# A chunked RWKV-5 mixer with a normalised MLP: r loaded four tokens a partition and turned for four batches at once, k turned alone by DMA, loads issued from two queues

## The chip, the cores and the metric

The kernel runs on one core of a Trainium2 chip. That core has a matrix engine (TensorE, PE in the profile; PEld is its loading of weights), three engines for elementwise work (VectorE or DVE, ScalarE or ACT, GpSimd or POOL), a queue engine (SyncE, SP) and 16 DMA engines. The metric is the device time of one launch in microseconds (us), the median of several runs.

## What is computed

Inputs are r, k and v of shape (4 batches, 8 heads, 768 tokens, 48), a decay w and a bonus u per head and dimension, and two matrices of an MLP that widens 384 to 1536 and back. The reference, cut to what matters:

```python
for t in range(S):
    cur = einsum('bhd,bhe->bhde', u * k[t], v[t])
    y[t] = einsum('bhd,bhde->bhe', r[t], state + cur)
    state = w * state + einsum('bhd,bhe->bhde', k[t], v[t])
...
mu, var = mean(x), mean((x - mu)**2)          # x is y with the heads side by side
xn = (x - mu) / sqrt(var + 1e-6) * g_ln
out = x + maximum(xn @ w_ch1, 0) @ w_ch2
```

The output is (4, 768, 384) in float32.

## The kernel before

The 768 tokens are cut into six chunk rows of 128. A tile is one chunk of one batch, 128 tokens by 8 heads by 48; there are 24, and tile i is chunk row i // 4 of batch i % 4. Inside a chunk the recurrence becomes matrix products: with r of token t scaled by w^t and k by w^-(t+1), the product of the scaled k and r, masked to earlier tokens, weighs v; the state Z at the start of the chunk is multiplied by the scaled r; and the token's own term comes from u.

The steps of a tile, by the names in the code:

- LR, LK, LV load r, k, v of a tile (L326, L323, L329), tokens on the partitions. One piece of memory is the 48 numbers of one head of one token, 192 bytes.
- SR and SK scale r and k by the tables Fr and Fk (tile `sc` in the profile); CV casts v to bf16 (`vv`).
- The scaled r and k must be turned, so that the dimension lies on the partitions (`trs`). Tiles 0 to 7 do it on PE: TR (L345) makes eight 128x128 transposes, four of r and four of k, into PSUM (`tr`), and TCr and TCk, or TC for both, copy them out. Tiles 8 to 23 do it by one DMA transpose of r and k together, TKR (L490).
- Q multiplies the turned r and k (`q`). AT (L364) forms the products (`at`), AM masks them (`A`). S computes the token's own weights (L395), for tiles 4 to 7 adds the old state by an identity matmul (L402), and makes the state product (L408); ZU and ZD make the next state Z. CC copies the own weights (`cc`), VB multiplies v by them (`Vb`). Y sums the state's part (L437) and the masked part (L445); X adds Vb (`x`) and gives the row sum.
- SQ and RS make the norm's factor, XN the centred rows (`xn`). They are turned for the MLP (`xT`): tiles 0 to 5 by LT on PE (L505) and a copy XT, tiles 6 to 19 two at a time by a DMA transpose LT2 (L484), the last four by LTD (L480).
- UP (L520) is a quarter or half of a widening product into one of two PSUM buffers (`hp`), RL (L536 on ACT, L538 on DVE) the relu out of it (`hT`). MLP groups have one or two tiles; a UP of one tile has 12 matmuls of 128 columns, of two tiles 6 to a matmul group of 256 columns. DN (L548) is a third of the narrowing product, four matmuls of 384 columns (`o`). OT adds x, STO stores. The last tile's narrowing is made in halves (DA, DB, L563).
- LW1, LW2 load the two weight matrices in thirds (`w_f`, L298 and L315; LW2 n into the buffer of LW1 n), SW scales and casts the first, CW casts the second.

At the start WF loads w to all partitions, LN takes its logarithm, FR and FK make the tables by exponentials, and WL makes the decay of a whole chunk, again by a logarithm and an exponential. TL (L229) loads in advance an activation table set named for both functions. DU and WU are matmuls on zeros that keep PE busy (L261, L265); a DU of n lasts as long as n matmuls of 128 columns.

The order is one written list, PLAN: each entry is a step, its number, and its engine (v DVE, s ACT, g POOL; for a DMA s means issued by ACT and - by SP). Every engine runs its entries in that order, and each waits only for its data and for its buffers. Tiles of one name form a ring (SLOTS: `kf`, `rf` and `vf` have eleven buffers each). In the list before, SP issues 123 DMAs, all loads among them; ACT issues 11.

Of the kernel before, what the change touches and what calls it, by code (L numbers as in the profile page):

```python
# [7 lines left out]
FP32 = mybir.dt.float32  # L8
BF16 = mybir.dt.bfloat16
ALU = mybir.AluOpType  # L10
# [5 lines left out]
K_BY_DMA = [8, 9, 10, 11, 12, 13, 14, 15, 16, 17, 18, 19, 20, 21, 22, 23]  # L16
SLOTS = {'kf': 11, 'rf': 11, 'vf': 11, 'sc': 3, 'vv': 4, 'trs': 3, 'q': 2, 'A': 2, 'cc': 4, 'Z': 6, 'ZS': 2, 'Vb': 3, 'x': 13, 'xn': 4, 'xT': 4, 'hT': 4, 'ot': 4}
PLAN = """
MP,0,v LR,1,- WF,0,s MW,0,v MI,0,g LR,0,- MM,0,g TL,0,s LC,1,- LK,0,- LV,0,- LN,0,s FR,0,s LC,0,s LR,2,- LK,1,- LC,2,s
SR,0,v FK,0,s SK,0,v LK,3,- DU,40,- CT,0,- TR,0,- CV,0,v LK,2,- SR,1,v TCr,0,s CP,0,v TCk,0,v UW,0,g LV,1,- UGC,0,s WL,0,s  # L20
DU,6,- AT,0,- Q,0,v SK,1,v S,0,- LW1,0,- SR,2,v TR,1,- LV,2,- CC,0,s SK,3,g AMb,0,v LR,3,- TCr,1,s AMa,0,v ZU,0,v VB,0,g
TCk,1,v DU,4,- Y,0,- SK,2,g CV,1,s DU,3,- AT,1,- X,0,v LW1,1,- Q,1,g AMb,1,v TR,2,- LW1,2,- AMa,1,v TCk,2,s LV,3,- DU,10,-
S,1,- TCr,2,s XN,0,v SW,2,v SW,0,s DU,5,- AT,2,- LR,4,- CC,1,v Q,2,v Y,1,- AMb,2,v LT,0,- CV,2,s VB,1,g SQ,0,s XT,0,v
SW,1,g X,1,v ZU,1,v SR,3,g XN,1,s DU,26,- UP,0,- AMa,2,v LT,1,- S,2,- RL,0,s SW,5,g XT,1,v ZU,2,v SW,3,s DU,5,- TR,3,-
Y,2,- LK,4,- RS,0,g CC,2,v SW,4,v TCr,3,s VB,2,v DU,4,- UP,1,- X,2,v SW,7,s LW2,0,- SW,6,g UP,17,- TCk,3,v LV,4,- RL,1,s
XN,2,v AT,3,- SW,8,s Q,3,v LW2,1,- UP,16,- CV,3,v RL,17,s LW2,2,- S,3,- SR,4,g RL,16,v DU,2,- UP,2,- LK,5,- AM,3,v CC,3,s
SQ,1,s SK,4,g LT,2,- UP,18,- XT,2,s RL,2,s ZU,3,v RS,1,g TR,4,- LR,5,- RL,18,s VB,3,v UP,34,- CW,1,s TC,4,v CW,0,g Y,3,-
UP,32,- X,3,v CV,4,s AT,4,- Q,4,v RL,32,s DN,4,- AM,4,v XN,3,g RL,34,s S,4,- LR,6,- SQ,2,s LT,3,- UP,33,- CC,4,v XT,3,v
CW,3,s VB,4,v Y,4,- RL,33,v UP,49,- CW,2,s X,4,v UP,50,- CW,4,s LK,6,- XN,4,v DN,5,- CW,5,v RL,49,s LR,7,- LT,4,- SK,5,v
RL,50,s DN,6,- XT,4,v SR,5,v UP,48,- LV,5,- OT,1,v TR,5,- SK,6,v ZU,4,v LK,7,- SR,6,g DN,0,- TC,5,s DN,1,- LV,6,- AT,5,-  # L30
Q,5,g TR,6,- LV,7,- AM,5,v UP,64,- DN,2,- TC,6,s LR,8,- CV,5,g SR,7,v RL,48,s AT,6,- S,5,- LR,9,- OT,0,v SQ,4,s SK,7,g
Y,5,- CC,5,s RL,64,s DN,8,- LK,8,- AM,6,v VB,5,g TR,7,- RS,2,g LK,9,- UP,65,- UP,66,- Q,6,v TC,7,s X,5,v ZU,5,v DN,9,-
CV,7,g LV,8,- RL,66,s CV,6,g AT,7,- SQ,3,s RS,4,g XN,5,v LV,9,- Q,7,v S,6,- SR,8,v LT,5,- LR,10,- DN,10,- ZU,6,v SK,8,g
CC,6,s SQ,5,s RL,65,s XT,5,v Y,6,- STO,0,s AM,7,v S,7,- UP,81,- VB,6,g TKR,8,- LK,10,- SK,9,g OT,2,v UP,80,- CC,7,v X,6,v
SR,9,g DN,16,- RL,80,v XN,6,s Y,7,- CV,8,s RS,5,g DN,17,- VB,7,v TKR,9,- RL,81,s STO,1,- X,7,v CV,9,g DN,18,- ZU,7,v SQ,7,s
XN,7,g UP,82,- OT,4,v Q,8,g LT2,6,- AT,8,- RL,82,s DN,20,- LK,11,- AM,8,v LR,11,- SK,10,g S,8,- DN,21,- CC,8,s RS,3,g Y,8,-
SR,10,v AT,9,- LV,10,- TKR,10,- DN,22,- VB,8,g UP,97,- OT,5,v Q,9,g LR,12,- UP,100,- ZU,8,v RL,97,s X,8,v DN,12,- SK,11,g SQ,6,s
AM,9,v LK,12,- S,9,- RL,100,s SR,11,g XN,8,s UP,99,- DN,13,- STO,2,- CC,9,s RL,99,s RS,6,g VB,9,v TKR,11,- Y,9,- ZD,8,v LV,11,-
AT,10,- UP,96,- ZU,9,v Q,10,g X,9,v DN,14,- RL,96,v UP,98,- XN,9,g OT,3,v CV,10,s LT2,8,- UP,101,- RL,98,s AM,10,v SK,12,g STO,3,-
DN,28,- LR,13,- S,10,- Q,11,v DN,29,- RL,101,v CC,10,s VB,10,g CV,11,s AT,11,- ZU,10,v LK,13,- LV,12,- Y,10,- SR,12,g AM,11,v DN,30,-  # L40
UP,115,- TKR,12,- X,10,v S,11,- LR,15,- RL,115,s UP,116,- CC,11,v OT,7,v XN,10,s VB,11,g LK,14,- Y,11,- RL,116,v DN,24,- SR,13,g X,11,v
CV,12,s SQ,8,s UP,112,- UP,117,- SQ,9,s XN,11,g RL,117,v ZD,9,g LT2,10,- DN,25,- RL,112,v LR,14,- AT,12,- SK,13,g LV,13,- DN,26,- UP,113,-
Q,12,v TKR,13,- ZU,11,v SK,14,g UP,114,- RL,113,s LK,15,- STO,4,- OT,6,v S,12,- RL,114,s UP,132,- CC,12,v SQ,11,s VB,12,g DN,32,- LV,14,-
RL,132,s RS,7,g SR,14,v UP,128,- UP,133,- SQ,10,s AM,12,v LV,15,- ZD,11,g DN,33,- RL,128,s LK,16,- Q,13,v AT,13,- STO,5,s ZD,10,v DN,34,-
RL,133,s SK,15,g ZU,12,v Y,12,- CV,13,s TKR,14,- UP,129,- OT,8,v SR,15,g X,12,v S,13,- LR,16,- DN,36,- CC,13,v CV,14,s AM,13,v ZU,13,v
UP,131,- TKR,15,- XN,12,s RL,131,s RL,129,s SQ,12,s DN,37,- STO,6,- VB,13,g ZD,12,g Y,13,- RS,8,g DN,38,- CV,15,v X,13,v UP,130,- OT,9,v
XN,13,s AT,14,- Q,14,v RL,130,s DN,40,- LT2,12,- AM,14,v SQ,13,s SR,16,g LV,16,- S,14,- DN,41,- LK,17,- CC,14,s STO,7,s ZU,14,v RS,9,g
Y,14,- SK,16,v AT,15,- Q,15,v DN,42,- TKR,16,- AM,15,v ZD,14,g VB,14,g S,15,- LR,17,- UP,149,- CC,15,s ZD,13,g OT,10,v UP,145,- RL,149,s
LR,18,- X,14,v VB,15,g DN,44,- RL,145,v XN,14,s UP,148,- ZU,15,v CV,16,s LV,17,- Y,15,- SQ,14,s DN,45,- SK,17,v RL,148,s LK,18,- X,15,v
AT,16,- ZD,15,g DN,46,- SQ,15,s UP,144,- Q,16,v XN,15,s OT,11,v SR,17,g UP,147,- RL,144,s LT2,14,- AM,16,v S,16,- UP,146,- TKR,17,- CV,17,g  # L50
STO,9,- RL,147,v DN,52,- RL,146,s LK,19,- SK,18,v Y,16,- CC,16,s LR,19,- ZU,16,v DN,53,- SR,18,v UP,161,- ZD,16,v DN,54,- VB,16,v RL,161,s
# [600 lines left out]
```

## Time and profile before

| | before |
|---|---|
| median of 3 runs | 154.89 us (153.79 to 155.48) |
| profiled execution: span from first to last instruction | 156.2 us |
| busy PE, DVE, POOL, ACT | 139.4, 112.9, 87.9, 75.1 us |
| DMA packets | 104465, of which 99579 under 512 bytes |
| first UP | 20.46 us |
| granted clock of PE | 1.00 throughout |

The span is that of one profiled execution; the runs are timed without a profile, and no other time is given for the profiled one. A group of the profile names line, engine, operation and tiles, then the count, the busy time, the mean in ns, and the idle time before it with what ended it. The chain of waits follows the last instruction back to what released it; SPq and ACTq stand for time in which a queue was issuing. A matmul's busy time overlaps that of its neighbours, so the distance from one start to the next is what a step costs when PE streams.

### The profile page before, as it was taken

How to read it: one execution, taken by the hardware profiler on the slowest of the kernel's cores; microseconds unless marked ns; L12 is line 12 of the kernel's file. 1: busy time of each engine (PE TensorE's matmuls, PEld its weight loads, DVE VectorE, ACT ScalarE, POOL GpSimd, SP SyncE). 2: the span in 40 equal slices, each digit the busy share in tenths (PEclk: the TensorE clock that was granted, in tenths of full speed). 3: DMA queues.
4: the chain of work that ended last, by engine and by line, in shares of the span. 5: the costliest groups of instructions: out<-in, count | busy, mean ns of one | idle time of the engine just before them, and what ended most of it. 6: DMA issues, size and time to landing. Idle time of an engine off the chain costs nothing.

```text
span 156.2 us, 4227 instructions
## 1 busy us (share of the span) xinstructions
PE 139.4 (89%) x1676; PEld 106.5 (68%) x1676; DVE 112.9 (72%) x224; ACT 75.1 (48%) x167; POOL 87.9 (56%) x127
## 2 busy tenths in 40 slices
PE   5659998999999869969969989998997999979991
PEld 1146687886778558757947767786775777758881
DVE  2149899996989856957659998899786767644421
ACT  3424666993766317135736547344253446615130
POOL 3016596503889979639739885134929885651000
PEclk9999999999999999999999999999999999999999
DMA  4999999988999979989989999999999898831221
GB/s 86 201 211 274 265 310 254 408 171 164 203 191 189 235 142 241 162 186 234 176 196 228 225 175 203 176 215 175 213 217 183 200 221 181 186 110 54 76 84 67
DMA packets 104465, 30.03 MB, mean 192 GB/s; under 512 B 99579, under 2 KB 102910, under 8 KB 104446
## 3 DMA queue, kind: packets, MB, share of 16 engines
q1 hardware_dynamic: 103132, 28.09, 89.4%
q10 hardware_dynamic: 1314, 1.67, 3.4%
q8 instruction: 13, 0.21, 0.6%
q14 instruction: 6, 0.05, 0.1%
HBM read 19.08 MB, written 4.72 MB: 152 GB/s over the span
## 4 chain that ended last, share of the span: by engine, by line
PE 29%; DMA 26%; SPq 21%; DVE 9%; POOL 5%; issue 4%; ACT 4%; ACTq 1%; DVEq 0%; POOLq 0%
PE hp L520 10%; PE o L548 9%; DMA xT<-xn 8%; DMA rf<-in_r_dram 8%; SPq L326 7%; SPq L329 5%; SPq L323 4%; DMA out_dram<-ot 3%; DMA w_all<-in_w_dram 2%; DMA kf<-in_k_dram 2%; DVE A L374 2%; POOL sc L194 2%; PE at L364 2%; PE o L261 2%; PE y L445 1%
## 5 line engine op out<-in xcount | busy, mean ns | idle before, releaser
L520 PE MATMUL hp<-xT,w_sb 128*128 128x128 bf16 (+1 forms) x612 | 57.1, 241 | 3.5 <-DMA xT<-xn 3.4
L548 PE MATMUL o<-w_sb,hT 128*128 128x384 bf16 x276 | 55.4, 326 | 0.6 <-DVE ot L604 0.4
L520 PEld LDWEIGHTS <-w_sb 128*128 128x128 bf16 x612 | 48.7, 114 | 8.4 <-DMA xT<-xn 3.2
L536 ACT ACTIVATE hT<-hp 128x512 bf16<-128x512 f32 x54 | 31.6, 595 | 34.4 <-PE hp L520 34.2
L548 PEld LDWEIGHTS <-hT 128*128 128x128 bf16 x276 | 24.2, 97 | 12.0 <-issue 0.8
L374 DVE TENSOR_TENSOR A<-at,mask 128x1024 bf16<-128x1024 f32 (+1 forms) x27 | 29.5, 1099 | 2.4 <-PE at L364 2.3
L194 POOL TENSOR_TENSOR sc<-kf,Fk 128x384 bf16<-128x384 f32 x15 | 15.4, 1026 | 14.9 <-DMA kf<-in_k_dram 9.0
L194 POOL TENSOR_TENSOR sc<-rf,Fr 128x384 bf16<-128x384 f32 x15 | 15.5, 1035 | 12.2 <-DMA rf<-in_r_dram 12.2
L604 DVE SCALAR_TENSOR_TENSOR ot<-o,rs,x 128x384 f32<-128x384 f32 x23 | 14.1, 614 | 8.7 <-PE o L548 4.3
L452 DVE SCALAR_TENSOR_TENSOR x<-y,Vb 128x384 f32<-128x384 f32 x24 | 13.2, 551 | 4.2 <-PE y L445 2.8
L427 POOL TENSOR_TENSOR Vb<-vf,cc 128x384 f32<-128x384 f32 x15 | 12.8, 850 | 6.0 <-DVE cc L191 4.3
L459 ACT ACTIVATE sqj<-x,sm 128x384 bf16<-128x384 f32 x24 | 14.7, 613 | 1.9 <-DVE x L452 1.8
L538 DVE TENSOR_SCALAR hT<-hp 128x512 bf16<-128x512 f32 x18 | 12.3, 686 | 3.1 <-PE hp L520 2.8
L364 PE MATMUL at<-trs 48*128 48x128 bf16 x192 | 10.0, 226 | 3.0 <-DMA trs<-sc 2.5
L476 POOL TENSOR_TENSOR rs<-rs,expo 128x1 f32<-128x1 f32 (+1 forms) x17 | 11.0, 649 | 1.4
L364 PEld LDWEIGHTS <-trs 48*128 48x128 bf16 x192 | 5.6, 97 | 8.6 <-DMA trs<-sc 3.9
L261 PE MATMUL o<-warm 128*128 128x512 bf16 x23 | 9.4, 533 | 2.0 <-DVE warm L226 2.0
L189 ACT CAST vv<-vf 128x384 bf16<-128x384 f32 x13 | 6.6, 509 | 9.2 <-DMA vf<-in_v_dram 7.8
L194 DVE TENSOR_TENSOR q<-trs 128x512 bf16<-128x512 bf16 x16 | 8.9, 555 | 2.6 <-DMA trs<-sc 2.5
L189 ACT COPY trs<-tr 128x512 bf16<-128x512 bf16 (+1 forms) x8 | 5.9, 747 | 9.3 <-PE tr L345 7.6
L194 POOL TENSOR_TENSOR q<-trs 128x512 bf16<-128x512 bf16 x8 | 9.6, 1196 | 0.9 <-PE hp L520 0.8
L445 PE MATMUL y<-vv,A 128*128 128x48 bf16 x192 | 8.8, 185 | 0.6 <-ACT vv L189 0.4
(76 smaller groups left out, 168.2 us busy)
## 6 DMA issues: line engine op xcount, KB each, us to landing
rf<-in_r_dram SPq DMA_DIRECT2D x24, 192.0 KB, 3.6
kf<-in_k_dram SPq DMA_DIRECT2D x24, 192.0 KB, 4.0
vf<-in_v_dram SPq DMA_DIRECT2D x24, 192.0 KB, 4.3
w_f<-in_moe_w_ch_dram SPq DMA_DIRECT2D x6, 768.0 KB, 6.1
out_dram<-ot SPq DMA_DIRECT2D x16, 192.0 KB, 3.6
out_dram<-ot ACTq DMA_DIRECT2D x7, 192.0 KB, 3.6
trs<-sc SPq DMA_TRANSPOSE x16, 3.5
w_all<-in_w_dram ACTq DMA_DIRECT2D x1, 192.0 KB, 3.8
```

Source lines behind the costliest of these rows:

```text
L189: nc.scalar.copy(out=out, in_=in_)
L194: engines[e].tensor_tensor(out=out, in0=in0, in1=in1, op=ALU.mult)
L261: nc.tensor.matmul(out=warm_ps[0][:], lhsT=warm[:], rhs=warm[:].unsqueeze(1).to_broadcast([P, 4, P]), start=True, stop=True)
L364: nc.tensor.matmul(out=t[:, par, q, :], lhsT=trs(i)[p0 : p0 + D, 1, q, :], rhs=trs(i)[p0 : p0 + D, 0, q, :], start=True, stop=True,)
L374: nc.vector.tensor_tensor(out=AA(i)[:, a:b].rearrange("p e q t -> p (e q) t"), in0=psum["at", i][:, a:b].rearrange("p e q t -> p (e q) t") ...
L427: engines[e].tensor_tensor(out=Vb(i)[:].rearrange("p (h d) -> p h d", h=H), in0=vf(i)[:], in1=cc(i)[:].unsqueeze(2).to_broadcast([P, H, D] ...
L452: nc.vector.scalar_tensor_tensor(out=xx(i)[:], in0=psum["y", i][:, :C], scalar=1.0, in1=Vb(i)[:], op0=ALU.mult, op1=ALU.add, accum_out=sm[ ...
L459: nc.scalar.activation(out=sqj[:], in_=xx(i)[:], func=ACT.Square, bias=sm[i][:], scale=-float(C), accum_out=sq[g][:, j : j + 1])
L520: nc.tensor.matmul(out=t[:, a * gw : (a + 1) * gw].rearrange("p (j t) -> p j t", j=size), lhsT=w1_sb[n][kc][:, fb::FB], rhs=xT(g)[:, :size ...
L536: nc.scalar.activation(out=o, in_=s, func=ACT.Relu)
L548: nc.tensor.matmul(out=psum["o", i][:, :C], lhsT=hT(g)[:, fk, j * P : (j + 1) * P], rhs=w2_sb[d][:, a, :], start=(fk == 0), stop=(fk == FK ...
L604: nc.vector.scalar_tensor_tensor(out=ot(i), in0=psum["o", i][:, :C], scalar=rs[g][:, j : j + 1], in1=xx(i)[:], op0=ALU.mult, op1=ALU.add,)
```

## The change

For chunk rows 1 to 5 (R_PACKED), r of the four batches of a row goes into one tile `rp`. LRP loads one batch into every fourth partition, four successive tokens of a head as one piece of 768 bytes. Four SRP scale it, two heads at a time over all four batches, by a new table Fr4, which FR4 makes in four exponentials out of `pow4`, the token numbers that MP4 computes on POOL in four small operations. Two TRP of eight transposes turn a whole row of r: the identity is read with a step of four, so that the batches come out apart; two TCP copy the result out of PSUM and put the tokens in order, into `rT`. k is scaled by SK as before and turned alone: on PE by TK (four transposes) for tiles 4 to 7, by TKD, one DMA transpose a tile, for tiles 8 to 23. Q, AT and Y read r from `rT` and k from `trk`. Row 0 keeps LR, SR and TR.

Loads may now be issued by ACT. The parts of a narrowing product may come in any order. The rings change: `kf` and `vf` 10, `rf` 4, `rp` 1, `rps` 1, `rT` 2, turned k 6, scaled k 6. The whole PLAN is new; its list gives SP 65 DMAs and ACT 69 (19 LK, 16 LV, 10 LRP, 3 LR, 3 LW1, 2 LW2, 13 STO and three more). The table load TL stands at the end of the list instead of near its start. On DVE, ACT and POOL some steps change places as well.

```diff
-K_BY_DMA = [8, 9, 10, 11, 12, 13, 14, 15, 16, 17, 18, 19, 20, 21, 22, 23]
+R_PACKED = [1, 2, 3, 4, 5]
...
+MI,0,g MP4,0,g MM,0,g WF,0,s MW,0,v LK,0,s LR,0,s LK,1,s DU,40,- LC,2,- MP,0,v DU,4,- DU,2,- LC,0,- LR,1,s LN,0,s FR,0,s FK,0,s SR,0,v SK,0,v LR,2,-
+LC,1,- LK,2,s LV,1,s TR,0,- CT,0,- FR4,0,s DU,6,- CP,0,s TCk,0,v SK,1,g LR,3,s TCr,0,v DU,5,- DU,3,- SR,1,v Q,0,v UW,0,g SR,2,g LV,0,- AT,0,- WL,0,s
+CV,0,s AMb,0,v AMa,0,v TR,1,- TCk,1,v S,0,- SK,2,v LRP,6,- LK,4,s TCr,1,s Q,1,v LW1,1,s AT,1,- TR,2,- Y,0,- FR4,1,s CC,0,s FR4,2,s LK,3,- CV,1,g
+ZU,0,v AMb,1,v VB,0,g FR4,3,s S,1,- TCk,2,v SR,3,g SK,3,g AMa,1,v TCr,2,s LV,2,- X,0,v ZU,1,v CC,1,s LRP,5,- AT,2,- Y,1,- VB,1,g TR,3,- LW1,0,s
...
+DA,2,- STO,22,- OA,23,v SA,23,s TL,0,s
...
+    def rTq(i, q):
+        return rT(i // B)[:, q, i % B, :] if i // B in R_PACKED else trr(i)[:, q, :]
...
+    def FR4(j, e):
+        nc.scalar.activation(out=Fr4[:, :, j, :], in_=ln_all[:], func=ACT.Exp, scale=pow4[:, j : j + 1])
...
     def LK(i, e):
-        nc.sync.dma_start(out=kf(i)[:], in_=chunk_src(k, i))
+        issuer(e).dma_start(out=kf(i)[:], in_=chunk_src(k, i))
...
+    def LRP(i, e):
+        c, b = divmod(i, B)
+        issuer(e).dma_start(
+            out=rp(c)[:].rearrange("(p b) h x -> b p h x", b=B)[b],
+            in_=r[b, :, c * L : (c + 1) * L, :].rearrange("h (p j) d -> p h (j d)", j=PK),
+        )
+
+    def SRP(i, e):
+        c, q = divmod(i, HP)
+        times(
+            e,
+            rps(c)[:, q].rearrange("p j (e x) -> p e j x", e=2)[:, :, :, :D],
+            rp(c)[:, 2 * q : 2 * q + 2].rearrange("p e (j d) -> p e j d", j=PK),
+            Fr4[:, 2 * q : 2 * q + 2],
+        )
+
+    def TRP(i, e):
+        c, h = divmod(i, 2)
+        t = psum["trp", i] = ps.tile([P, HP // 2, PK, P], BF16, name="tr")
+        for a in range(HP // 2):
+            for j in range(PK):
+                nc.tensor.transpose(
+                    out=t[:, a, j, :], in_=rps(c)[:, h * (HP // 2) + a, j, :],
+                    identity=ident[:].rearrange("k (n b) -> k b n", b=B),
+                )
+
+    def TCP(i, e):
+        c, h = divmod(i, 2)
+        n = HP // 2
+        copy(
+            e, rT(c)[:, h * n : (h + 1) * n].rearrange("p q b t -> p q (b t)").rearrange("p q (m j) -> p q j m", j=PK),
+            psum["trp", i][:],
+        )
...
-    def TKR(i, e):
...
     def TKD(i, e):
-        flat = sck(i).rearrange("p h d -> p (h d)")
-        nc.sync.dma_start_transpose(out=trs(i)[:, 1], in_=flat)
+        nc.sync.dma_start_transpose(out=trk(i), in_=sck(i).rearrange("p h d -> p (h d)"))
```

More of the change, by code (lines that the diff above doesn't have):

```diff
@@ new lines @@
+LRP,7,- LT,1,- SW,5,g S,2,- XT,1,v CC,2,v AT,3,- LK,7,s SRP,4,v SRP,5,v AM,3,v LT,0,- LV,3,- VB,2,g UP,17,- XT,0,s ZU,2,v X,2,v TRP,2,- Q,3,g SRP,6,v
+UP,1,- TCP,2,s XN,2,s CV,3,g TK,4,- LK,5,- LK,6,- TCk,4,v LT,2,- S,3,- RL,17,s SW,1,s CC,3,s Y,3,- SRP,7,v XT,2,v SW,0,v LV,5,s TRP,3,- RL,1,v SW,2,g
+VB,3,g UP,32,- UP,0,- SK,5,v SW,8,v RL,0,v TCP,3,s TK,5,- AT,4,- RL,32,s SW,7,g SW,6,s SK,6,g AM,4,v UP,16,- LRP,11,s TCk,5,s X,3,v UP,18,- ZU,3,v
+RL,16,s LRP,10,s TK,6,- TCk,6,s RL,18,s Q,4,g LW2,0,s LW2,2,s LV,4,- CV,4,g AT,5,- UP,33,- S,4,- Y,4,- SK,7,g TK,7,- AM,5,v LW2,1,- AT,6,- CC,4,v
@@ L125 @@
     vf = ring("vf", [P, H, D], FP32)
[L126 removed]
     vv = ring("vv", [P, H, D], BF16)
[L128 removed]
+    scr = ring("scr", [P, H, DP], BF16)
+    trr = ring("trr", [P, HP, P], BF16)
+    sck2 = [const.tile([P, 2, H, DP], BF16, name=f"sck{a}") for a in range(SLOTS["sck"] // 2)]
+    trk2 = [const.tile([P, 2, HP, P], BF16, name=f"trk{a}") for a in range(SLOTS["trk"] // 2)]
+    rp = ring("rp", [P, H, PK * D], FP32)
+    rps = ring("rps", [P, HP, PK, E2 // D * DP], BF16)
+    rT = ring("rT", [P, HP, B, P], BF16)
     qq = ring("q", [P, HP, P], BF16)
@@ L341, in TR, with TK, ATP @@
         t = psum["tr", i] = ps.tile([P, 2 * HP, P], BF16, name="tr")
-        for a, s in enumerate((scr,) if i in K_BY_DMA else (scr, sck)):
-            flat = s(i).rearrange("p (q e) d -> p q (e d)", e=2)
+        for a, s in enumerate((scr(i)[:], sck(i))):
+            flat = s.rearrange("p (q e) d -> p q (e d)", e=2)
             for q in range(HP):
                 nc.tensor.transpose(out=t[:, a * HP + q, :], in_=flat[:, q, :], identity=ident[:])
+    def TK(i, e):
+        t = psum["tr", i] = ps.tile([P, 2 * HP, P], BF16, name="tr")
+        flat = sck(i).rearrange("p (q e) d -> p q (e d)", e=2)
+        for q in range(HP):
+            nc.tensor.transpose(out=t[:, HP + q, :], in_=flat[:, q, :], identity=ident[:])
     def TCr(i, e):
-        copy(e, trs(i)[:, 0], psum["tr", i][:, :HP])
+        copy(e, trr(i)[:], psum["tr", i][:, :HP])
     def TCk(i, e):
-        copy(e, trs(i)[:, 1], psum["tr", i][:, HP:])
-    def TC(i, e):
-        copy(e, trs(i)[:], psum["tr", i][:].rearrange("p (a q) t -> p a q t", a=2))
+        copy(e, trk(i), psum["tr", i][:, HP:])
     def Q(i, e):
-        times(e, qq(i)[:], trs(i)[:, 0], trs(i)[:, 1])
+        times(e, qq(i)[:], rTall(i), trk(i))
+    def ATP(i, e):
+        for a in (i, i + 1):
+            AT(a, e)
     def AT(i, e):
```

155 lines of the change are left out of this document (79 added, 76 removed).

## The prediction, made before the result was known

> **What bounds the kernel now.** I read the page first: busy times, queues, the chain that ended last.
>
> ```profile
> span 156.2 us, 4227 instructions
> ...
> PE 139.4 (89%) x1676; PEld 106.5 (68%) x1676; DVE 112.9 (72%) x224; ACT 75.1 (48%) x167; POOL 87.9 (56%) x127
> ...
> q1 hardware_dynamic: 103132, 28.09, 89.4%
> q10 hardware_dynamic: 1314, 1.67, 3.4%
> ...
> PE 29%; DMA 26%; SPq 21%; DVE 9%; POOL 5%; issue 4%; ACT 4%; ACTq 1%; DVEq 0%; POOLq 0%
> ```
>
> PE is nearest to full, but 47% of the chain is transfers and SP's issuing of them. The busy time by stage (PE, PEld, DVE, ACT, POOL, clock, DMA share, GB/s), cut at 47 us, where the last state product with L402 (tile 7) runs, and at 138 us, where tile 23's L395 starts:
>
> ```profile
> 0.00:47.00 47.00, 41.05 (x528) 30.11 (x529) 35.78 (x83) 27.89 (x56) 23.52 (x43) 1.00 0.93 228
> 47.00:138.00 91.00, 84.38 (x983) 64.97 (x980) 71.11 (x131) 42.84 (x103) 62.47 (x82) 1.00 1.08 200
> 138.00:157.00 19.00, 14.02 (x174) 11.42 (x171) 6.04 (x12) 4.37 (x9) 1.87 (x4) 1.00 0.18 61
> ```
>
> DMA is full until 138 us; ACT is half idle. PE's busy time hides stalls, so I price its work by the chain, which shows steps as they follow each other, and by the PE timeline:
>
> ```profile
> 47.42 1.50 PE L520 MATMUL hp<-xT,w_sb 128*128 128x128 bf16 x24
> ...
> 9.61 0.98 PE tr L345 x8
> 59.64 0.66 PE hp L520 x6
> 60.29 0.65 PE o L548 x4
> 85.17 0.17 PE y L437 x4
> 85.33 0.20 PE y L445 x8
> 86.84 0.33 PE at L364 x8
> 87.93 0.08 PE s L395 x4
> 88.01 0.20 PE s L408 x4
> 145.17 0.67 PE hp L520 x12
> 152.42 0.34 PE hp L563 x4
> ```
>
> I call the end of tile 7's S at 47.42 us **the mark**. The order before holds behind it 15 UP of one tile (0.67 each), 42 of two (0.66), 60 DN (0.65), six half DNs (0.33), 16 AT (0.33), 17 Y (0.37) and 16 S (0.28, the last four 0.08): 10.1 + 27.7 + 39.0 + 2.0 + 5.3 + 6.3 + 3.7 = 94.1 us. PE ends at 152.76, so it took 105.3: **11.2 us of stall**, then 3.4 us to the span's end.
>
> Where the stalls come from, by the waits, and what SP did, by its timeline and groups:
>
> ```profile
> POOL sc L194 <- DMA rf<-in_r_dram: 12.2, 7, 6.4
> POOL sc L194 <- DMA kf<-in_k_dram: 9.0, 4, 5.2
> PEld L364 <- DMA trs<-sc: 3.9, 5, 1.6
> PE hp L520 <- DMA xT<-xn: 3.4, 3, 1.2
> ...
> 25.84 7.39 SPq L326 DMA_DIRECT2D rf<-in_r_dram  x2
> ...
> L490 SPq DMA_TRANSPOSE trs<-sc x16: 1232/1506/2782, 47.3 to 130.8; - x16
> L326 SPq DMA_DIRECT2D rf<-in_r_dram x24: 425/582/4276, 0.7 to 122.5; - x24
> L611 ACTq DMA_DIRECT2D out_dram<-ot x7: 338/338/376, 46.6 to 147.8; - x7
> ```
>
> Loads and transposes come late since one queue issues 123 of them; at 25.84 us two r loads held SP for 7.39 us.
>
> **The change, part by part.**
>
> *DMA engines.* q1's packets took 0.894 x 16 x 156.2 / 103132 = 21.7 ns each, q10's 64.7 (mean 1.27 KB). A packed r tile is 256 pieces of 768 B instead of 1024 of 192 B. Over 20 tiles 20480 packets go (444 us of engine time) and 5120 come, at 21.7 to 64.7 ns: 111 to 331 us. On 16 engines that saves 7 to 21 us; I take 10, low, as 21.7 holds the slower transposes. Turning k alone halves what 16 transposes move, a few us more. So the DMA share falls from 1.08 to between 0.95 and 1.0. Nothing of this enters the sum by itself; it shortens stalls.
>
> *Issuing.* SP's list falls from 123 to 65. ACT's rises from 11 to 69. Each of the 58 costs ACT between 0.34 us (its own stores) and 0.58 (SP's median r load); I take 0.45, near SP's shortest r load, 0.43: 26 us. Queued behind each are the hT evictions that free PE's two hp buffers.
> [...]
>
> *ACT's other work.*
>
> ```profile
> L189 ACT COPY trs<-tr 128x1024 bf16<-128x1024 bf16 x3 | 3.0, 1013 | 3.7 <-PE tr L345 2.1 <-DVE Z L194 1.6
> L229 ACT ACT_TABLE_LOAD x1 | 1.3, 1283 | 1.2 <-PEq L636 1.2
> L277 ACT ACTIVATE Fr<-ln_all,pow_i 128x384 f32<-128x384 f32 x1 | 0.6, 616 | 0.1
> ...
> 4.56 0.53 ACT L271 ACTIVATE ln_all<-w_all 128x384 f32<-128x384 f32 x1 [2.08 <-DMA w_all<-in_w_dram]
> ```
>
> Nine TCP at 1.01 replace three TC: +6.1. Four FR4 of Fr's form: +2.5. TL, which loads the joint logarithm and exponential set in advance (L229), moves behind the last store. The build must then place loads itself: if it takes the joint set there is still one; if not, one at each change, LN to FR, then WL's logarithm and its exponential: three more, 3.9 us. I take three, since the explicit line would otherwise not be needed. The first is hidden under the 2.08 us wait for w_all; TL at the end lies beside the last store.
> [...]
>
> *PE.* A TR of 8 transposes took 0.44 us once PE streamed:
>
> ```profile
> 42.49 0.61 PE L345 MATMUL tr<-ident,sc 128*128 128x128 bf16 x8
> 42.93 1.50 PE L520 MATMUL hp<-xT,w_sb 128*128 128x128 bf16 x24
> ```
>
> Ten TRP at 0.44 come; four TR become TK at 0.22: +4.4 - 0.9 = +3.5 us. TRP streams the identity with a step of four, which the trace doesn't show: bounds 0.44 (no effect) and 0.98, what TR 0 took at 9.61; I take 0.44, the rate of a PE that streams. Behind the mark the new order has 66 DN, 17 single UP, 18 Y, eight TRP and one LT (0.17), the rest as before: 42.9 + 11.4 + 27.7 + 2.0 + 5.3 + 6.7 + 3.7 + 3.5 + 0.2 = **103.4 us**, 9.3 more: 3.5 of TRP, the rest UP and DN not yet done at the mark.
>
> *DVE and POOL.* SRP replaces SR one for one at the same size. Of the 48 scalings of r and k DVE now takes 27 instead of 18:
>
> ```profile
> L194 DVE TENSOR_TENSOR sc<-rf,Fr 128x384 bf16<-128x384 f32 x9 | 5.5, 606 | 4.9 <-DMA rf<-in_r_dram 4.9
> ```
>
> That is +5.5 us; what else it gains (CC, CW, TCk) and gives up (Q, VB, XN) about cancels, and at 72% it hides this. POOL loses the nine and gains Q and VB. MP4's four operations on one or four columns stand ahead of its first large work: nothing.
>
> *Weights at the start.*
>
> ```profile
> 9.89 0.81 SPq L298 DMA_DIRECT2D w_f<-in_moe_w_ch_dram  x1
> ...
> 20.46 0.83 PE L520 MATMUL hp<-xT,w_sb 128*128 128x128 bf16 x12
> ...
> w_f<-in_moe_w_ch_dram SPq DMA_DIRECT2D x6, 768.0 KB, 6.1
> ```
>
> LW1 moves to ACT behind WL, CV 0 and TCr 1, to about 16 us, with 6.1 to land and a scaling: the first UP comes at 23 to 24 instead of 20.46, and this is why UP and DN are pushed behind the mark.
>
> **When the mark comes.** By PE: from the first UP to the mark the new order has 13 UP (8.7), two TRP and four TK (1.8), three LT (0.5), S 3 to 7 (1.4, and four L402, each as wide as a matmul of DN, 0.7), Y 3 to 5 (0.9), AT 4 to 7 (1.3), three DN (2.0): 17.3 us behind 23.5, so 41 without a stall. By ACT:
>
> ```profile
> L536 ACT ACTIVATE hT<-hp 128x512 bf16<-128x512 f32 x54 | 31.6, 595 | 34.4 <-PE hp L520 34.2
> L459 ACT ACTIVATE sqj<-x,sm 128x384 bf16<-128x384 f32 x24 | 14.7, 613 | 1.9 <-DVE x L452 1.8
> L189 ACT CAST w_sb<-w_f 128x768 bf16<-128x768 f32 x4 | 3.2, 837 | 0.4 <-DMA w_f<-in_moe_w_ch_dram 0.4
> ```
>
> Of its 27.9 us in the first 47, five RL (3.0), two SQ (1.6 with their reads), two CW (1.7), one SW and three TC (3.7) and TL (1.3) go; two TCP (2.0), four FR4 (2.5), three XN and one trs copy (2.4) come: about 24 us up to CV 7, which the mark needs. Start at LN, 4.56 as before (WF is still first), add 15 issues behind LN (6.8) and three loads (3.9): 39.3 without one wait. ACT idled 19 us in that stage; with all of it the mark comes at 58, with none at 41, PE's bound. I take **45**, four of stall on PE's bound, since waits of ACT and PE now fall on each other: ACT is some 77% taken there, and it was 59%.
>
> **Sum.** Mark 45, work 103.4, stall 6.5 (of 11.2 goes the DMA part, near 7 by the two PE waits above; ACT adds some 2.2, a tenth of its 49 issues behind the mark), end 3.4: 158.3 us against the profile's 156.2. The runs' median, 154.89, lies 1.3 below that span, so **157.0 us**, 1.4% slower.
>
> **The rivals.**
>
> *Faster: SP and DMA were the only hold.* The chain's 47% speaks for it, and ACT's 48%. Then no table loads are added, ACT delays nobody (mark 42.5), and stall is 3: 42.5 + 103.4 + 3 + 3.4 - 1.3 = 151.0. Against it: ACT at 75 + 26 + 6 + 2.5 + 3.9, some 113 us, in order, and PE's 9.3 us more behind the mark.
>
> *Even: who issues hardly matters.* ACT pays only its own 0.34 an issue, so the mark comes at 44 and the stall it adds is under 1, 4.5 in all with a little left of DMA's: 44 + 103.4 + 4.5 + 3.4 - 1.3 = 154.0. [...]
>
> *Much slower: ACT stands as SP stood.* [...] Now ACT issues all LW1, two LW2 and 35 k and v loads, with hT evictions behind them. One hold as long as the longest of L326, 4.28 us, that no other wait covers puts the mark at 49.5; the 49 issues behind the mark 0.06 longer each give 3 more of stall, 9.5: 49.5 + 103.4 + 9.5 + 3.4 - 1.3 = 164.5. It decides from a hold of about 2 us on ACT between LW1 and CV 7. Against: less for DMA to do, and two queues.
>
> *TRP doesn't keep 0.44.* At 0.98 ten of them add 5.4 us to any of these; with the forecast's other terms 162.4.
>
> **Chances.** The forecast's case 0.46, its own range 153 to 161; faster 0.20; even 0.10; ACT held or TRP slow 0.24. About 1% is what a measurement can tell here. Below 153.3 lie the faster case and 0.05 of the forecast's and the even one: 0.25. Above 156.4 lie the last case and 0.29 of the forecast's: 0.53. Between: 0.22. The range 151.0 to 164.5 leaves out half of each outer case, about a fifth.
>
> **What would show it.** In the profile after: SPq falls to under 10% of the chain and ACT with ACTq rises; ACT busy near 87 us with three to four table loads; fewer than 90000 packets; first L520 at 23 to 24 us; the last L402 at 43 to 47 us; behind it PE stalls of 5 to 8 us, named by ACT's hT rather than by xT or trs. The forecast is wrong if ACT issues cost under 0.2 us, if the mark comes by 41 us, or if an issue on ACT lasts several us.

## The result and the profile after

The kernel after takes **181.41 us** (median of four runs, 179.20 to 182.26), the kernel before 155.19 beside it (153.79 to 156.33): **1.165 times** the time, 95% interval 1.154 to 1.175. Forecast were 157.0 and a range to 164.5. The change is much slower, and none of the written cases reaches this far. Medians are over all runs of a kernel; the ratios leave out a run that took over 1.5% more than the fastest of its kernel.

The page of the kernel after: its busy times, the clock of the 40 slices, the bytes moved, the chain of waits, and one group.

```profile
span 177.2 us, 4399 instructions
...
PE 151.4 (85%) x1740; PEld 117.3 (66%) x1740; DVE 121.0 (68%) x239; ACT 98.8 (56%) x175; POOL 89.5 (51%) x130
...
PEclk9965589699999999999999999999999999999999
...
PE 50%; DVE 17%; ACT 14%; DMA 8%; issue 7%; POOL 2%; ACTq 2%; DVEq 0%; POOLq 0%
PE o L614 18%; PE hp L584 16%; ACT rT L202 10%; PE tr L379 4%; DMA trk<-sck 4%; DMA kf<-in_k_dram 3%; DVE A L442 3%; PE at L432 2%; PE o L285 2%; DVE Z L207 2%; DVE sck L207 2%; PE y L513 2%; DMA vf<-in_v_dram 2%; DVE hT L602 1%; DVE rT L204 1%
...
L202 ACT COPY rT<-tr 128x1024 bf16<-128x1024 bf16 x9 | 22.2, 2466 | 10.6 <-PE tr L379 8.5
```

Look at the last row first. TCP, the copy of the turned r out of PSUM, takes 2466 ns for as many elements as the copy of 128x1024 that took 1013 in before, and it stands in the chain with 10%. SPq, 21% of the chain in before, is gone from it: the queue that the change was to relieve is relieved, and nothing is won. DMA isn't the limit any more either: it is 8% of the chain against 26%.

PE's transposes of the packed r (TRP), by their tile, and the way in which transpose and copy follow each other in the chain (start, us, what):

```profile
L379 PE MATMUL tr<-ident,rps x80: 274/296/298, 26.7 to 128.7; 128*128 128x128 bf16 x80
...
107.26 1.04 PE tr L379 x8
108.32 2.47 ACT rT L202
110.83 1.11 PE tr L379 x8
111.97 2.46 ACT rT L202
```

Eight transposes hold PE here for 1.04 to 1.11 us (0.93 to 1.11 over the chain), not 0.44, and the second half of a row waits for the copy of the first, since both use one PSUM tile: from the first transpose to the last copied element a row takes 7.2 us.

What became of the two sides of the mark, 10 to 50 and 50 to 150 us, by the windows (busy us of PE, PEld, DVE, ACT and POOL, then PE's granted clock, DMA's share, GB/s); before first, then after:

```profile
10.00:50.00 40.00, 38.64 (x564) 30.41 (x562) 35.68 (x76) 26.64 (x57) 24.94 (x34) 1.00 0.99 246
50.00:150.00 100.00, 92.32 (x1063) 71.04 (x1062) 72.79 (x133) 44.83 (x107) 61.34 (x82) 1.00 0.97 183
```

```profile
10.00:50.00 40.00, 34.45 (x457) 27.31 (x456) 32.50 (x69) 27.66 (x50) 24.41 (x31) 0.79 0.95 243
50.00:150.00 100.00, 87.22 (x983) 68.56 (x980) 74.12 (x136) 55.03 (x96) 54.69 (x70) 1.00 0.68 139
```

PE loses in both stages: 4.2 us of busy time in the first, where its clock is low besides (0.79 against 1.00; 107 multiplications fewer got done), and 5.1 in the second, where DMA fell from 0.97 to 0.68. With gaps on DMA and on PE alike, this stage is held by the chains of steps that run between them.

### The profile page after: what moved, and what is told of

Its sections match the earlier page's. It is cut to its first block, busy times and chain, and to the rows that moved or that the text cites. A ratio compares the mean times of both kernels' runs of the same rounds, so it can differ in the third digit from the quotient of the medians.

```text
span 177.2 us, 4399 instructions
## 1 busy us (share of the span) xinstructions
PE 151.4 (85%) x1740; PEld 117.3 (66%) x1740; DVE 121.0 (68%) x239; ACT 98.8 (56%) x175; POOL 89.5 (51%) x130
## 2 busy tenths in 40 slices
DMA packets 80913, 27.93 MB, mean 158 GB/s; under 512 B 70907, under 2 KB 79358, under 8 KB 80894
## 4 chain that ended last, share of the span: by engine, by line
PE 50%; DVE 17%; ACT 14%; DMA 8%; issue 7%; POOL 2%; ACTq 2%; DVEq 0%; POOLq 0%
PE o L614 18%; PE hp L584 16%; ACT rT L202 10%; PE tr L379 4%; DMA trk<-sck 4%; DMA kf<-in_k_dram 3%; DVE A L442 3%; PE at L432 2%; PE o L285 2%; DVE Z L207 2%; DVE sck L207 2%; PE y L513 2%; DMA vf<-in_v_dram 2%; DVE hT L602 1%; DVE rT L204 1%
## 5 line engine op out<-in xcount | busy, mean ns | idle before, releaser
L495 POOL TENSOR_TENSOR Vb<-vf,cc 128x384 f32<-128x384 f32 x18 | 15.3, 852 | 28.1 <-DVE cc L204 17.7
L202 ACT COPY rT<-tr 128x1024 bf16<-128x1024 bf16 x9 | 22.2, 2466 | 10.6 <-PE tr L379 8.5
L672 DVE SCALAR_TENSOR_TENSOR ot<-o,rs,x 128x384 f32<-128x384 f32 x23 | 14.1, 612 | 12.5 <-PE o L614 12.4
L207 POOL TENSOR_TENSOR q<-rT,trk 128x512 bf16<-128x512 bf16 x10 | 12.2, 1219 | 17.2 <-ACT rT L202 6.8
L207 POOL TENSOR_TENSOR sck<-kf,Fk 128x384 bf16<-128x384 f32 x12 | 13.0, 1086 | 5.7 <-DVE scr L207 5.7
L379 PE MATMUL tr<-ident,rps 128*128 128x128 bf16 x80 | 11.1, 293 | 3.5 <-ACT rT L202 3.4
L432 PE MATMUL at<-rT,trk 48*128 48x128 bf16 x160 | 8.5, 219 | 4.1 <-DMA trk<-sck 1.8
L379 PEld LDWEIGHTS <-rps 128*128 128x128 bf16 x80 | 8.6, 112 | 4.9 <-issue 4.0
L432 PEld LDWEIGHTS <-trk 48*128 48x128 bf16 x192 | 6.0, 98 | 8.7 <-issue 5.3
L541 POOL TENSOR_SCALAR rs<-sq 128x1 f32<-128x1 f32 (+1 forms) x17 | 3.9, 229 | 13.0 <-ACT sqj L527 11.8
L207 POOL TENSOR_TENSOR rps<-rp,Fr 128x384 bf16<-128x384 f32 x7 | 8.2, 1178 | 3.3 <-DMA rp<-in_r_dram 3.3
```

The source lines that it names most:

```text
L202: nc.scalar.copy(out=out, in_=in_)
L207: engines[e].tensor_tensor(out=out, in0=in0, in1=in1, op=ALU.mult)
L379: nc.tensor.transpose(out=t[:, a, j, :], in_=rps(c)[:, h * (HP // 2) + a, j, :], identity=ident[:].rearrange("k (n b) -> k b n", b=B),)
L432: nc.tensor.matmul(out=t[:, par, q, :], lhsT=trk(i)[p0 : p0 + D, q, :], rhs=rTq(i, q)[p0 : p0 + D, :], start=True, stop=True,)
L495: engines[e].tensor_tensor(out=Vb(i)[:].rearrange("p (h d) -> p h d", h=H), in0=vf(i)[:], in1=cc(i)[:].unsqueeze(2).to_broadcast([P, H, D] ...
L672: nc.vector.scalar_tensor_tensor(out=ot(i), in0=psum["o", i][:, :C], scalar=rs[g][:, j : j + 1], in1=xx(i)[:], op0=ALU.mult, op1=ALU.add,)
```

## The experiments

Times are medians; "before" stood at 157 to 158 beside all of these runs, and the ratios are to that. They ran on several chips, and one kernel differed between two of them by 0.8 and 1.0 us (the kernel after and e12, e5 and e14). e1 to e4 have two runs each and wide intervals, so what the terms are worth rests on e12 to e14, which share a chip.

### The copy

```diff
 (e2)  copy(e, rT(c)[...] "p q (m j) -> p q j m",        psum["trp", i][:])
  ->   copy(e, rT(c)[...] "p q (m j) -> p q m j",        psum["trp", i][:] "p q j m -> p q m j")
 (e1)  copy(e, rT(c)[...] "p q b t -> p (q b t)",        psum["trp", i][:] "p q j m -> p (q j m)")
```

In the kernel after the copy reads PSUM in order and writes rT in steps of four tokens, 8 bytes. e2 turns this round: the same elements, PSUM read in steps, rT written in order. e1 reads and writes in order and so leaves out the reordering of the tokens.

e1:

> Only TCP changes: it writes rT in the order in which PE left the tokens, contiguous on both sides, so the putting in order of the tokens is left out. Theory A (the copy's writes with a step of four tokens cost 2.47 us instead of 1.0, on ACT in order, and hold the one tr buffer): a TCP takes 1.0 us, the ten save 14.5 us, and 10 to 15 us of it come off the end: 165 to 171 us. Rival B (the new order and the start decide, the copies stand in the shadow of other waits): TCP gets short, but the time falls by less than 4 us, 177 or more.

e2:

> TCP walks the tokens in their order: it reads PSUM with a step of 128 elements and writes rT contiguously; everything is computed. If only writes with a step are slow, TCP takes about 1.0 us and the time is that of the plain copy, 165 to 171 us by theory A. If reads of PSUM with a step are as slow, TCP stays near 2.4 us and the time near 180 us.

171.07 and 170.11 us (ratio of e2 1.082, 1.045 to 1.120): the upper end of theory A's times, and on ACT the two copies cost the same, 1012 ns. Repeated beside the kernel after on one chip (e12, e13):

> The kernel after itself, beside its steps on one chip. 181.4 on another chip, against before's 155.2 there; before stood at 157 to 158 on the chips of the other runs, so 181 to 185.

> The kernel after with the copy of r alone mended (as in e2), beside the kernel after on the same chip. If the copy is the largest part: 10 to 12 us below the kernel after. If other steps take up its gain: under 6.

180.60 and 170.15: **10.4 us** by the medians, 9.7 by the ratios (1.147 and 1.085). The group of e13:

```profile
L202 ACT COPY rT<-tr 128x1024 bf16<-128x1024 bf16 x9 | 9.1, 1012 | 10.6 <-PE tr L379 8.5 <-POOL rs L541 2.1
```

1012 ns, what the forecast took: on ACT, reading PSUM in steps costs nothing here, and writing in steps of 8 bytes cost 1.45 us a copy. ACT's nine copies give 13.1 us back. DVE makes the tenth; in the kernel after:

```profile
L204 DVE COPY rT<-tr 128x1024 bf16<-128x1024 bf16 x1 | 2.4, 2434 | 1.6 <-PE tr L379 1.6
```

It took 1224 ns with the reads in steps (e2) and 691 with both sides in order (e1): on DVE the step costs on either side, less on the reading one. Of the 14.3 us that the ten copies give back 10.4 arrive at the end: most of it was in the open.

### The transposes and the table loads

```diff
 (e3)  identp[k, (b n)] = ident[k, (n b)]     # copied once at the start, by POOL
       nc.tensor.transpose(out=t[:, a, j, :], in_=..., identity=ident[:].rearrange("k (n b) -> k b n", b=B))
  ->   nc.tensor.transpose(out=t[:, a, j, :], in_=..., identity=identp[:])
 (e4)  PLAN: ... WF,0,s TL,0,s MW,0,v ...     # TL from the end to the start
```

> TRP streams an identity that is put in order once at the start by one copy on POOL, without a step of four. If the step is what made a TRP take 0.91 to 1.09 us, it falls to 0.44 to 0.5 and PE's own work falls by about 5 us. Where PE bounds, 4 to 5 us come off: 175 to 177 us. Where the copies behind TRP bound (theory A), PE only waits longer for the tr buffer: 178 to 181 us.

> TL stands behind WF again instead of at the end: one table load instead of four at the start. ACT is 3.9 us less busy before 15 us. If ACT's start decides, tile 7's S ends at 46 to 47 us instead of 50.0, and 3 to 4 us come off: 176 to 178 us. If the copies and the order decide, 0 to 1 us: 179 to 181 us.

177.57 and 179.89 (ratios 1.130 and 1.145): e3 lies between its two cases, e4 in the one in which copies and order decide. Single transposes fell from 296 to 219 ns in e3; in e4 the five table loads of the kernel after (four at the start, TL at the end, 1283 ns each) became one, and the mark moved from 50.0 to 49.4. Both together with e2's copy, twice, the second time on the chip of e12 and e13:

> The kernel after, with three edits at once: the copy of r reads PSUM in steps and writes in order (179 to 170 when tried alone), the identity put in order once (179 to 177.6 when tried alone), TL moved forward to behind WF (nothing that could be told when tried alone). Theory A (the price of the copy and of the transposes is most of the loss, and both add): 170.1 - 3.8 - 0.7 = 165 to 166, with the eight transposes of an item at 0.5 us from one start to the next and the last L470 at 46 to 47. Rival B (order and issuers: these prices were partly hidden behind waits that the order makes): 168 to 170, the reductions do not add. Under both some 9 to 12 us above before stay unexplained.

> The kernel after with copy, identity and TL mended (as in e5), beside the two above on the same chip. If the parts add: 4 to 5 us below the run with the copy alone; if they overlap: 2 to 3.

167.40 and **166.41** (ratio of e14 1.061, 1.051 to 1.070): 3.7 us below e13, between the two cases written down for it. The transposes in e14:

```profile
L383 PE MATMUL tr<-identp,rps x80: 217/219/315, 24.8 to 123.6; 128*128 128x128 bf16 x80
```

So on one chip: 180.6, less 10.4 for the copy, less 3.7 for identity and table loads, leaves 9.1 us above before (157.3).

### What is left: clock, issuers, order, late transposes

```diff
 (e6)  three + "DU,40,-" ahead of TR,0          (dummies against an idle PE)
 (e7)  three, LK LR LV LW of ACT all issued by SP
 (e9)  e6 + SK and TKD of tiles 8 to 11 some 40 to 60 steps earlier
 (e8, e10)  the operations of three in before's order, all loads by SP, TRP/TCP put where SRP has ended
```

> The kernel of the run with three edits, with 40 more dummy multiplications (DU) ahead of the first transposes, where TensorE stands idle for 3 us while it waits for the first loads, so that it isn't idle before the clock is granted. Theory C (the low granted clock of 0.5 to 0.8 between 10 and 40 us costs time by itself): the clock of those slices comes to 0.9 or more, and the time falls by 3 to 5 us against the run with three edits. Rival (TensorE waits for others there anyway, its clock costs nothing): within 1 us of it. If the idle window isn't closed by 40 of them, the clock in 10 to 20 us stays at 0.5 and the run says nothing.

> The kernel of the run with three edits, with every load of chunk rows and weights issued by SP, as in before, instead of in part by ScalarE. Theory D (ScalarE's share of the loads delays its copies and the first steps): ScalarE is freed of some 50 issues at 0.45 us, 22 us, LN comes 4 us earlier, and the time falls by 3 to 8 us. Rival (SP with its transposes by DMA becomes the longer queue): the same or up to 5 us more, with SPq in the chain of waits as it was in before.

e6 165.47, beside e5's 167.40 on its chip: the clock of 10 to 20 us rose only from 0.50 to 0.70, the mark didn't come earlier (46.7 against 45.7), and the runs overlap. The pause that the dummies were to fill was 1.26 us in e5, not 3, and 0.71 in e6; that such a pause sets the clock was an assumption of mine, which no run shows. Theory C's clock of 0.9 wasn't reached and the fall of 1.9 us lies between the two cases, so the price of the low clock stays open here. e7 173.02 (ratio 1.092, e5's 1.063): SP becomes the longer queue, as the rival said. The first 50 us, e5 and then e7, whose profile is of its run of 174.59 us:

```profile
0.00:50.00 50.00, 40.98 (x522) 30.28 (x523) 39.20 (x91) 27.96 (x56) 28.26 (x50) 0.86 0.95 232
0.00:50.00 50.00, 33.51 (x395) 24.55 (x396) 28.56 (x69) 22.62 (x45) 21.68 (x41) 0.80 0.87 221
```

PE is busy 33.5 us against 41.0, with SPq for vf, kf and rp at the head of that stage's chain (18, 17 and 15%). So the second issuer is worth some 5 us in this order (5.6 by the medians, 4.5 by the ratios) and isn't what makes the change slow.

> The kernel of the run with three edits and the added dummies, with SK and TKD of tiles 8 to 11 moved forward in the order (about 40 to 60 steps each), so that their transposes by DMA are issued before PE needs them instead of beside it; LK 8 and LK 11 are moved forward to match. In the run with three edits two of these transposes took 3.65 us from 48.17 and 6.66 us from 54.11 in the chain of waits, and DMA moved 4 to 112 GB/s from 41 to 49. Theory G (the stall left behind the mark is the transposed k of chunk row 2 that comes too late, because SK of these tiles stands late on DVE and POOL): the waits for trk there go and the time falls from 165.5 to 160 to 162. Rival H (PE is then held by DVE or ACT instead, both near full from 38 to 52 us): within 1.5 us of 165.5, with the wait of PE moved to hT, A or rT.

164.44, 1 us below e6, on another chip: the rival H. The transposes that stood in the chain for 6.66 us are out of it, and DVE stands there instead, busy 10.0 of 10 us from 40 to 50, as it already was in e5.

> The operations of the change (r of rows 1 to 5 loaded four tokens a partition, turned by TensorE for four batches at once; k of 16 tiles turned by DMA one by one) with the two mended prices and TL ahead, but in the order and with the issuers of before: each step of before stays where it was, the new steps take the place of those they replace, SP issues the loads. Theory E (what is left of the loss beside the two prices is the new order with its issuers): 152 to 158, the time of before or less, the granted clock at 0.97 or more. Rival F (the operations themselves cost more than those they replace: 24 single transposes of k on the queue, TensorE's added transposes): 162 or more, with waits on the transposed k or on rT.

172.27. Part of r of rows 3 to 5 was scaled before the last of its four loads, a slip in the order; the amount of work is the kernel's. (The transposes of k by DMA are 16, not 24.) Mended:

> The operations of the change in the order and with the issuers of before, as in e8, now with the last load of each of three chunk rows of r ahead of the scaling that reads it (in e8 that scaling read part of r before it was loaded; the work was the same). Theory E fell with e8 at 172: nothing that this run moves is on a theory's path, so both expect 170 to 174; under 165 would say that e8's time came from the slip.

**166.97**, outside what was written for it; I can't say how much of the 5 us between the two is the slip and how much the other chip. That it isn't under 162 stands against theory E: before's own order and issuers give the change no better time than its new ones (166.41 in e14). The packed loads stand mostly four tiles ahead of before's, and the rings aren't the kernel's (`rp` 2, scaled and turned k 4), so order and issuers aren't all that differs. Where that order loses, by the chain of e10:

```profile
12.69 3.58 SPq L353
...
17.61 7.84 DMA w_f<-in_moe_w_ch_dram
```

SP issues packed r of row 1 (L353, LRP) ahead of the first weights, and the first of the two loads holds it for 3.58 us; the weights behind them take 7.84 us to land, and PE is busy 10.1 us of the 15 from 20 to 35.

### PE's added work

```diff
 (e11, the kernel before)  for q in range(HP):  ->  for q in list(range(HP)) * (2 if i >= 8 else 1):   # in AT
```

> The kernel before, with the eight multiplications of AT (48x128 by 128) issued twice for tiles 8 to 23: 128 short multiplications more, spread as the transposes of r by TensorE are spread in the kernel after, 16 x 0.33 = 5.3 us of PE at the rate of 0.33 an AT in the chain of waits; the result is the same. Theory J (PE bounds before, so that what the change adds to it, 64 transposes net at 0.09 us, 6 us, is lost in full, and this is what remains once the two prices are mended): the time rises by 4.5 to 6 us, to 161 to 163. Rival K (before's 11 us of stall behind the mark take them up): the time rises by under 2 us, and what remains of the loss is the new waits.

**158.81** against 157.33, ratio 1.011 (1.004 to 1.019). PE in e11:

```profile
PE 142.4 (91%) x1804; PEld 110.1 (70%) x1804; DVE 112.2 (71%) x224; ACT 75.3 (48%) x167; POOL 87.9 (56%) x127
```

Its busy time rose from 139.4 to 142.4, 3.0 us and not the 5.3 expected, the time by 1.5. That is rival K's time, but half of the added busy time does arrive. PE is busy 146.4 us in e14 and 142.9 in e17; at that rate its added work would be some 3.5 of e14's 9 us and 1.8 of e17's 5 (below), an estimate. The 64 added transposes aren't the whole of the remaining 9 us.

### Row 1 left as it was, and the lead of the packed loads

```diff
  R_PACKED = [1, 2, 3, 4, 5]  ->  [2, 3, 4, 5]   # row 1: LR, SR, TR per tile, as in before; order and issuers of before
 (e15, e16, e17)  each LRP three, five, six tiles ahead of the place of before's LR
 (e18)  e16 with DU,40 -> DU,56
```

> The operations of the change for chunk rows 2 to 5 only, with the two mended prices and TL ahead, in the order and with the issuers of before; r of row 1 is loaded tile by tile and turned with k by TensorE as in before, and each load of packed r comes three tiles ahead of the place that before's load of the same number had. Theory L (what remains of the loss is that a packed row needs the r of four batches before its first tile can start, and that this falls in the first 40 us, where DMA is full: there PE was busy 33 us of 40 from 10 to 50 against 38.6 in before): PE is busy 37 to 38.6 us from 10 to 50 again, and the time comes to 157 to 161. Rival M (the remainder lies behind the mark, in the transposes and new waits of rows 2 to 5): PE from 10 to 50 comes back or not, and the time stays at 163 to 167.

> As e15 (row 1 as before, rows 2 to 5 packed, the order and issuers of before), with each packed load five tiles ahead instead of three; in e15 POOL and DVE waited 24.6 us for rp, with everything of POOL's list behind it. Theory L (the packed row needs the lead; given it, the remainder of the loss goes, since row 1 no longer front-loads): the waits for rp fall under 8 us and the time to 157 to 162. Rival M (every lead that hides the packed loads takes the place of loads that PE needs sooner): 163 to 170, with waits on weights, k or v in place of those on rp.

> As e16, six tiles ahead. Theory L: within 2 us of e16, the lead being there already. Rival M: later than e16 by 1 to 4 us, since more loads stand ahead of the weights.

181.37, 170.00 and **162.84** (ratios 1.154, 1.079, and 1.031 with 1.020 to 1.043). e15 lies outside both its cases, PE being busy only 31.6 us from 10 to 50; e16 is at the upper end of rival M's; e17, 7 us below e16, is in neither. Theory L's times didn't come, in e15 because the loads were late. POOL's waits for rp in e15 and in e16 (us in all, times, longest):

```profile
POOL rps L210 <- DMA rp<-in_r_dram: 20.1, 4, 6.4
```

```profile
POOL rps L210 <- DMA rp<-in_r_dram: 6.5, 1, 6.5
```

DVE waited 4.5 and 2.6 us besides. Two loads of rp are left in e16's chain, 3.90 us from 36.89 and

```profile
77.92 5.08 DMA rp<-in_r_dram
```

In e17 both are gone from the chain, and 0.2 us of waits for rp are left. Three tiles of lead more go with 18.5 us; the first two of them, with the clock of 10 to 20 us at 0.52 and 0.50, with 11.4. A packed row is usable only when all four of its loads are there, so its first tile waits for the fourth. The windows of e17:

```profile
10.00:50.00 40.00, 34.66 (x486) 26.87 (x484) 31.58 (x67) 26.57 (x56) 20.99 (x28) 1.00 0.96 254
50.00:150.00 100.00, 96.12 (x1167) 75.58 (x1166) 78.68 (x143) 53.55 (x121) 63.76 (x87) 1.00 0.74 155
```

Behind 50 us PE is now fuller than in before; what it still loses, 4.0 us, it loses between 10 and 50, where the earlier loads now stand.

> As e16, with four wide dummy multiplications more ahead of the first transposes (DU 40 to 56), in a gap of 2.61 us in which PE waits for the first rows; in e16 the granted clock was 0.50 from 10 to 20 us after that gap, in e17 with a gap of 2.50 us it was 1.00 throughout, and the two kernels differ in the lead of the packed loads alone. Theory C again (the low clock at the start costs time by itself, most of the 7 us between e16 and e17): the clock of 10 to 20 us is at 0.9 or more and the time falls to 162 to 165. Rival N (the lead of six tiles made e17's gain, or the clock pays nothing as in e6): the clock comes up and the time stays at 168 to 170.

168.82 (165.99 to 170.90; ratio 1.059), and the clock of 10 to 20 us rose only from 0.50 to 0.66, not to the 0.9 that both cases count on. The median fits rival N, but two of the four runs, 165.99 and 167.23, lie 2.5 to 4 us below e16's 169.72 to 170.02. So it isn't shown that the lead made all of the 7 us between e16 and e17; the clock, which was 1.00 in e17, may have a share. Nor does the lead alone order the runs: e10, with four tiles of it and five packed rows, took 3 us less than e16.

No version beats before; the best, e17, is about 5 us above it (5.3 by the medians).

## Why the prediction was wrong

- **Nine TCP at 1.01 replace three TC: +6.1.** This is the step that failed. Nine cost 22.2 us instead of 9.1, and the copy mended gave 10.4 of the 24 us between forecast and result. I bounded TRP's strided identity from both sides and didn't see that TCP's output has the same stride: the nearest row, the copy of 128x1024 at 1013 ns, had the size but not the form. The write with a step of 4 elements took 2466 ns, the one in order 1012 (e13).
- **Ten TRP at 0.44.** The choice was wrong: 0.93 to 1.11, about the upper bound of 0.98 and in part above it. With the identity in order the stride goes, and a TRP takes 0.45 in e10's chain. As a term: ten times 0.5 to 0.6, 5 to 6 us; identity and table loads together gave 3.7 on one chip (e13, e14).
- **Stall 6.5.** PE ends at 174.1, 124.1 us behind the mark at 50.0. With TRP at its measured price the work there is near 107, so the stall was 17. In e5 and e14, where copy and identity are as forecast, the mark is at 45.7 and 46.7, PE ends at 161.5 and 161.2, and 115.8 and 114.5 less 103.4 leave 12.4 and 11.1. The stall stayed what it was in before, 11.2: the term was 5 to 6 us too small even so. Of the part that was to go, PE's waits for xT went (3.4 us in before, 0.3 behind 50 us in e14), those of AT for a transposed k stayed (2.5 in both). The reason that was to add to it, waits of PE on ACT's hT, isn't seen; PE waits for DVE's hT, and in the kernel after for rT. There, over the whole run (us in all, times, longest):

```profile
PE tr L379 <- ACT rT L202: 3.4, 4, 1.0
...
PE hp L584 <- DVE hT L602: 3.2, 4, 1.3
...
PE at L432 <- DMA trk<-sck: 1.8, 1, 1.8
```

  And in its chain a single tile of k:

```profile
60.73 0.98 POOL sck L207
...
61.72 6.36 DMA trk<-sck
```

- **Mark 45.** 50.0 in the kernel after, where the copies and transposes of row 1 (6.5 us between 26.9 and 35.6 in its chain) moved it; 47.4 in e13, which has the forecast's copy and its table loads; 45.7 and 46.7 in e5 and e14, which have one table load. The working was 1 to 2 us short. First UP 25.39 against 23 to 24. With the stall this accounts for what the two mended prices leave: e14's span is 164.2 against the sum's 158.3, 1.7 by the mark, 4.6 by the stall, less 0.4 at the end.
- **Three more table loads, 3.9 us.** The build didn't make do with one: it placed four at the start, and TL made a fifth. The first was to be hidden under the wait for w_all and wasn't. ACT first issues four loads, one of which held it for 1.85 us, and LN starts behind the table load, at 6.19 and not at 4.56:

```profile
2.27 1.85 ACTq L350 DMA_DIRECT2D kf<-in_k_dram  x1
...
4.90 1.28 ACT L295 ACT_TABLE_LOAD   x1 [4.90 <-issue]
6.19 0.52 ACT L295 ACTIVATE ln_all<-w_all 128x384 f32<-128x384 f32 x1
```

  LN follows the end of the load at once, 6.18 and 6.19 us. Taken away (e4), the loads were worth 1.5 us at most.
- **Issuing.** SPq left the chain, ACT's issues cost 0.37 to 0.47 mostly, packets fell to 80913 (under 90000): right. ACT standing as SP stood isn't seen: behind the first four loads no single issue held it for more than 1.40 us. ACT's busy time was forecast as 87 and is 98.8; 13.1 of that are the copies.
- **DMA share 0.95 to 1.0.** 0.68 from 50 to 150 us. Less is to be moved (27.93 MB against 30.03), and it is asked for later: the transposes by DMA of tiles 8 to 23 are issued from 52.4 to 147.2 us, in before from 47.3 to 130.8.
- **From span to time.** I took 1.3 off the span. The kernel after's profiled run took 179.20 with a span of 177.2, 2.0 more, and before's runs took about 1.8 more than theirs (158.01 and 156.2): before's profiled execution was thus slower than all three timed runs, and the same sum should have been read as a ratio, 158.3 / 156.2, on 154.9. It gives 157.0 too, so this cost nothing.

**What stays open:** the last 5 us of e17 and the 9 of e14 have no single cause that a run took away. Shown is that the order and issuers of before don't remove them, and that in before's order a lead of five tiles in place of three takes 11 us off; the 7 us of the sixth tile came with a higher clock (1.00 against 0.50 from 10 to 20 us). That the rest is the price of needing four loads before a row's first tile is argued from the windows of 10 to 50 us, not shown.

## What to carry over

A copy or a multiplication is priced by its access pattern on both sides, not by its size (a copy of 128x1024 took 1012 ns on ScalarE written in order and 2466 in steps, a transpose 219 ns with the identity in order and 296 in steps): before an output with a step is taken at the price of one in order, put the step on the side that reads PSUM, which cost nothing here on ScalarE (1012 ns with and without) and 0.5 us on VectorE (1224 ns against 691). Packing several batches into one load saves packets (80913 here against 104465, with k turned alone besides), but it makes a tile wait for the slowest of several loads (POOL waited 20.1 us for rp in e15), so it needs a lead: of the three, five and six tiles tried here the longest, one and a half rows, was best (181.37, 170.00 and 162.84 us). The lead takes the place of other loads (in e10 packed r held SP for 3.58 us ahead of the first weights), and whether those were needed sooner has to be looked up in the first stage. When a change relieves the queue that the chain names, price first what it puts on the engine next to it.

## What the chip showed that was not expected

In some runs PE's granted clock fell to about half soon after a pause at the start, in others not, and the length of the pause doesn't tell which. The first rows of PE behind the pause, in the kernel after, in e16 and in e17 (start, us, engine, line, what, count, and the pause in brackets):

```profile
9.35 0.40 PE L406 MATMUL tr<-ident,scr 128*128 128x128 bf16 x4 [3.16 <-DVE scr L207]
```

```profile
9.27 0.36 PE L235 MATMUL s<-idr,rows 11*128 11x11 f32 x2 [2.61 <-DMA rows<-in_moe_g_ln_dram]
```

```profile
9.18 0.56 PE L235 MATMUL s<-idr,rows 11*128 11x11 f32 x2 [2.50 <-DMA rows<-in_moe_g_ln_dram]
```

The stretch from 10 to 20 us in e16 and in e17, the clock third from the end:

```profile
10.00:20.00 10.00, 8.08 (x79) 5.00 (x78) 8.19 (x16) 4.89 (x13) 5.23 (x7) 0.50 0.97 255
```

```profile
10.00:20.00 10.00, 8.80 (x98) 5.87 (x97) 8.16 (x18) 5.32 (x14) 5.50 (x8) 1.00 0.98 256
```

After 3.16 and 2.61 us the clock of 10 to 20 us was 0.50, in e14 after 1.84 as well; after 2.50, and after 2.64 in before, it was 1.00. With the pause cut to 0.71 (e6) and 0.65 (e18) it still was 0.70 and 0.66. What decides it no run here shows.

What the low clock costs isn't settled. Raising it in part by dummies went with 1.9 us in e6, whose runs overlap those of e5, and with 1.2 us by the medians in e18. The mean clock of a run doesn't order the times: e13 took 170.15 us at 0.946 and 170.08 at 0.988, e18 167.23 at 0.959 and 170.90 at 0.960.
